# A kernel in a written order: a new order table in which the query-weight products stand behind their landing

## The chip, the cores and the metric

The kernel runs on one core of a Trainium2 chip. The metric is the device time of one execution in microseconds; the time before is the median of seven runs. Times inside an execution are counted from the start of its profiled span.

## What is computed

There are 2048 tokens of 640 numbers. Two branches read the same `x`, and a gate per token mixes them:

```python
g = sigmoid((x * gate_w).sum(-1))            # one number per token
a = linear_attention(x, wqkv, w_phi) @ wo    # 32 heads of 20
b = (silu(x @ w_gate) * (x @ w_up)) @ w_down # 1728 hidden columns
out = g * a + (1 - g) * b
```

In the attention branch q and k of each head go through a 20x20 matrix `w_phi`; the features are the softmax of the result beside the softmax of its negative (40 per head). `kv` sums feature times v over all tokens, `z` sums the features, and the result is `(phi_q kv) / (phi_q z)`. Because the sum over tokens must be complete before the first query can be finished, all key work comes ahead of the query work.

## The kernel before, in words

Everything stays in SBUF. The work is cut into items of a few microseconds. `LOADS` (line 31) and `ORDER` (line 36) are two lists of such items, and the loop at line 735 runs through them and calls the function of each; this one list fixes the order of instructions on every engine at once. Each engine then works through its own instructions strictly in that order, and `_Tracker.run` (line 143) puts a semaphore wait ahead of an instruction where it needs a result of another engine or a buffer that another engine still uses. So moving an item in the table moves its part on PE, ACT, DVE, POOL and, where it issues a transfer, on SP.

The items, with what each does on each engine:

- `H`, `G`, `X`, `U`, `V`: warm-up, gate column, transposed tokens of tiles 0 to 3, and values of a token tile. `V` (line 479) is ten matmuls on PE and two copies on ACT.
- `k0..k4` and `q0..q4` in `LOADS`: transposing DMAs on SP of the key and query columns of `wqkv` into `wT` and `wTq` (line 385), one per block of 128 rows. `t4..t15` are transposing DMAs of `x` (line 371).
- `M m`: block m of the key weights times the block-diagonal `w_phi` (`premult`, line 552), six matmuls, then a copy on DVE (m even) or ACT (m odd). `R m`: the same for the query weights from `wTq`, its copy always on ACT.
- `K t`: key features of tile t: ten matmuls, two exponentials on ACT into one of four `ekr` buffers. `S t`: sums and reciprocals on DVE. `P t`: the multiplication on POOL. `E t`: eleven matmuls that add to `kv` in PSUM.
- `I` and `N`: between them `kv` holds one PSUM pair, so only three of the four pairs are in the ring. `N` evicts `kv` on DVE. `Z` spreads `z` over partitions, `J` makes the gates, `T` copies the last 64 gate and up columns on POOL, `L` issues the loads of `wd` and `wog` on SP. `i3` and `i4` are memsets on POOL (line 405).
- `Q t`: query features, ten matmuls and two exponentials into one of three `eq` buffers. `A`, `B`, `C`: sums and denominators on DVE. `c t` (line 630): the multiplication on POOL into `ph`, and a transposing DMA on SP into `phiT`.
- `F b.k`: gate and up products of a block of four tiles, for 128 hidden columns: ten matmuls of 512 columns (five for k = 13), tanh and a copy on ACT, one operation on DVE, one on POOL.
- `O b.p`: features times `kv`, copies on ACT. `D b.u`: the down product and the output product of one token tile, 38 matmuls, the scaled copy on ACT, the output transfer on SP.

PSUM results go through a ring of pairs of banks, the pair used longest ago first:

```python
def next_pair():
    return used([r for r in ring["lru"] if r < ring["n"] and r not in held][0])
```

An item on PE thus waits until the pair that it is given has been read by ACT and DVE. And a query weight product reads what its transposing DMA wrote:

```python
pairs.append((o, (wT if which else wTq)[:, m, c, :], wbd[:, c, off:off + c1 - c0], i in (0, 3), i in (2, 5), True))
```

so PE waits there for the landing of `q m`.

Of the kernel before, what the change touches and what calls it, by code (L numbers as in the profile page):

```python
# [34 lines left out]

ORDER = """
H0 H1 H2 H3 H4 H5 H6 H7 H8 G X0 H9 H10 H11 U0.0 X1 U0.1 U1.0 U1.1 X2 U0.2 U1.2 U2.0 U2.1 X3 U2.2
U0.3 U1.3 U2.3 U0.4 U1.4 U2.4 V3 Y i3 i4 F0.0 M0 M1 F0.1 V4 M2 M3 M4 K0 K3 K1 S0 K2 S1 V7 V9 S2 P0
I V5 E0 K4 V8 P1 E1 S3 S4 P2 K5 P3 E2 P4 S5 K6 P5 R2 E3 V6 S6 K7 E4 K8 S7 E5 V14 P6 K9 E6 S8 V10
S9 P7 K10 E7 R0 K11 R4 S10 P8 E8 P9 T S11 P10 F0.5 K12 V11 P11 S12 E9 R1 F1.12 E10 K14 K13 P12 S14  # L40
P14 S13 P13 E11 R3 K15 S15 V13 F1.8 P15 F0.8 V12 V15 E12 E13 E14 E15 Q1 Q0 Q2 N A0 F1.13 F0.4 Z A1
B0 J F0.3 B1 F0.13 F1.0 C0 F1.6 F1.2 L c0 F0.6 F1.10 C1 c1 B2 F0.12 F0.10 F0.2 F1.1 A2 F0.9 C2 c2
Q3 B3 F1.5 Q4 A3 C3 c3 Q5 F1.9 F0.7 Q6 A5 A4 F1.3 B5 F1.4 F1.11 B4 O0.2 F0.11 C4 O0.0 A6 O0.1 c4
C5 Q7 B6 c5 C6 B7 c6 A7 C7 Q8 c7 F1.7 D0.2 D0.1 D0.3 Q9 Q10 D0.0 B9 O1.0 O1.1 O1.2 B8 A10 A8 A9 C8
c8 F2.5 F2.13 C9 Q11 F2.11 B10 c9 F2.12 C10 F2.0 D1.3 F2.6 A11 F2.1 F2.7 B11 F2.9 c10 Q12 Q13 A12
C11 c11 A13 F2.4 D1.2 F2.10 D1.0 Q14 B12 D1.1 O2.0 B13 C13 C12 O2.1 O2.2 c12 F3.12 A14 F3.0 F3.7
F3.4 F3.9 F3.13 F3.10 c13 Q15 F2.3 B14 A15 F2.2 F2.8 C14 F3.6 B15 C15 F3.8 F3.1 D2.2 F3.11 F3.5
c15 c14 F3.2 D2.0 D2.1 O3.0 O3.2 O3.1 F3.3 D2.3 D3.0 D3.2 D3.1 D3.3
"""


# [731 lines left out]
```

## Time and profile before

| | before |
|---|---|
| median of 7 runs | 292.06 us (291.61 to 294.35) |
| the profiled execution, its own time | 292.7 us |
| its span | 291.5 us |
| granted TensorE clock | 1.000 |
| PE matmul, busy | 286.5 us, 98% |
| DVE, ACT, POOL, busy | 159.3, 147.9, 161.3 us |
| SP's transposing loads of wTq, issued | 31.2 to 37.8 us |

PEld in the profile is the loading of matmul weights, which overlaps the matmuls. SPq is the queue of transfers that SP issues. "Idle before" is the time that an engine stood still ahead of an instruction, with the releaser behind an arrow. Since matmul records overlap, the time from the start of one item to the start of the next is the better measure of what an item costs PE.

### The profile page before, as it was taken

How to read it: one execution, taken by the hardware profiler on the slowest of the kernel's cores; microseconds unless marked ns; L12 is line 12 of the kernel's file. 1: busy time of each engine (PE TensorE's matmuls, PEld its weight loads, DVE VectorE, ACT ScalarE, POOL GpSimd, SP SyncE). 2: the span in 40 equal slices, each digit the busy share in tenths (PEclk: the TensorE clock that was granted, in tenths of full speed). 3: DMA queues.
4: the chain of work that ended last, by engine and by line, in shares of the span. 5: the costliest groups of instructions: out<-in, count | busy, mean ns of one | idle time of the engine just before them, and what ended most of it. 6: DMA issues, size and time to landing. Idle time of an engine off the chain costs nothing.

```text
span 291.5 us, 4872 instructions
## 1 busy us (share of the span) xinstructions
PE 286.5 (98%) x1975; PEld 174.8 (60%) x1975; DVE 159.3 (55%) x242; ACT 147.9 (51%) x252; POOL 161.3 (55%) x124
## 2 busy tenths in 40 slices
PE   8999989999999999999999999999999999999997
PEld 5667767675744455546775464567545455656776
DVE  1257667756677769859919793659243691100000
ACT  1358667875675557572534824543456543234112
POOL 7684977969137896765540674742345834811000
DMA  7996798000562221302360220051210200340101
GB/s 222 191 107 120 110 246 316 7 1 2 189 177 52 49 52 27 72 2 49 59 158 25 52 47 26 2 97 47 49 26 0 52 0 22 21 126 0 47 22 48
DMA packets 48777, 21.28 MB, mean 73 GB/s; under 512 B 39346, under 2 KB 48754, under 8 KB 48754
## 3 DMA queue, kind: packets, MB, share of 16 engines
q1 hardware_dynamic: 47368, 20.25, 30.9%
q10 hardware_dynamic: 1386, 0.71, 0.9%
q8 instruction: 16, 0.26, 0.4%
q14 instruction: 7, 0.06, 0.1%
HBM read 8.96 MB, written 2.62 MB: 40 GB/s over the span
## 4 chain that ended last, share of the span: by engine, by line
PE 86%; SPq 11%; DMA 1%; issue 0%; DVE 0%
PE ps L294 86%; SPq L347 10%; DMA wTq<-in_A_wqkv_dram 1%; SPq L348 1%; DVE osb L712 0%
## 5 line engine op out<-in xcount | busy, mean ns | idle before, releaser
L322 POOL TENSOR_TENSOR hT<-hT,us 128x512 bf16<-128x512 bf16 (+1 forms) x56 | 68.2, 1226 | 60.3 <-DVE hT L326 58.4
L326 DVE SCALAR_TENSOR_TENSOR hT<-hT,ps 128x512 bf16<-128x512 bf16 (+1 forms) x56 | 38.2, 684 | 69.8 <-ACT hT L312 66.3
L294 PE MATMUL ps<-xT,wg 128*128 128x512 bf16 x260 | 64.6, 379 | 0.0
L294 PE MATMUL ps<-xT,wu 128*128 128x512 bf16 x260 | 64.6, 379 | 0.0
L294 PE MATMUL ps<-wd,hT 128*128 128x320 bf16 (+2 forms) x462 | 63.9, 295 | 0.0
L312 ACT ACTIVATE hT<-ps 128x512 bf16<-128x512 f32 (+2 forms) x60 | 35.7, 595 | 45.9 <-PE ps L294 45.7
L322 POOL TENSOR_TENSOR ph<-eq,qc 128x1320 bf16<-128x1320 bf16 x16 | 40.8, 2552 | 32.0 <-DVE qc L625 29.9
L294 PEld LDWEIGHTS ps<-wd,hT 128*128 128x128 bf16 x462 | 44.5, 98 | 17.7
L294 PE MATMUL ps<-wqk,xT 128*128 128x320 bf16 x320 | 47.1, 299 | 0.0
L294 PEld LDWEIGHTS ps<-xT,wu 128*128 128x128 bf16 x260 | 25.5, 98 | 30.7
L322 POOL TENSOR_TENSOR ekr<-ekr,krec 128x1280 bf16<-128x1280 bf16 x16 | 37.5, 2357 | 8.5 <-DVE krec L336 8.1
L294 PEld LDWEIGHTS ps<-xT,wg 128*128 128x128 bf16 x260 | 25.0, 98 | 28.7 <-issue 1.7
L312 ACT ACTIVATE osb<-ps,omg 128x640 bf16<-128x640 f32 (+2 forms) x17 | 12.9, 758 | 57.0 <-PE ps L294 57.0
L294 PEld LDWEIGHTS ps<-wqk,xT 128*128 128x128 bf16 x320 | 30.6, 98 | 13.1 <-ACT hT L312 0.4
L312 ACT ACTIVATE us<-ps 128x512 bf16<-128x512 f32 (+1 forms) x56 | 33.2, 593 | 0.1
L333 DVE TENSOR_REDUCE ksum<-ekr 128x64 f32<-128x1280 bf16 x16 | 23.4, 1464 | 12.8 <-ACT ekr L312 12.8
L312 ACT ACTIVATE eq<-ps 128x640 bf16<-128x640 f32 x32 | 22.3, 703 | 16.0 <-POOL ph L322 11.1
L294 PE MATMUL ps<-wvg,xT 128*128 128x320 bf16 (+1 forms) x160 | 25.3, 306 | 0.4 <-DMA wvg<-in_A_wqkv_dram 0.3
L312 ACT ACTIVATE ekr<-ps 128x640 bf16<-128x640 f32 x32 | 22.2, 703 | 6.6 <-PE ps L294 6.1
L333 DVE TENSOR_REDUCE qz<-eq 128x64 f32<-128x1280 bf16 x16 | 23.4, 1478 | 2.6 <-ACT eq L312 2.6
L294 PE MATMUL ps<-wog,oT 128*128 128x320 bf16 (+2 forms) x165 | 24.7, 295 | 0.0
L333 DVE TENSOR_REDUCE qw<-ez 128x64 f32<-128x1280 bf16 x16 | 23.6, 1478 | 0.1
(73 smaller groups left out, 184.4 us busy)
## 6 DMA issues: line engine op xcount, KB each, us to landing
out_dram<-osb SPq DMA_DIRECT2D x15, 160.0 KB, 1.8
wd<-in_B_w_down_dram SPq DMA_DIRECT2D x1, 2080.0 KB, 9.3
wg<-in_B_w_gate_dram SPq DMA_DIRECT2D x1, 1040.0 KB, 10.6
wu<-in_B_w_up_dram SPq DMA_DIRECT2D x1, 1040.0 KB, 12.7
wg<-in_B_w_gate_dram SPq DMA_DIRECT2D x1, 800.0 KB, 6.3
wu<-in_B_w_up_dram SPq DMA_DIRECT2D x1, 800.0 KB, 8.3
wog<-in_A_wo_dram SPq DMA_DIRECT2D x2, 375.0 KB, 7.0
wvg<-in_A_wqkv_dram SPq DMA_DIRECT2D x4, 160.0 KB, 3.7
```

The lines of the kernel that those rows point to most:

```text
L294: last = pe.matmul(o, lhsT=l, rhs=r, start=st, stop=sp_, skip_group_check=sk)
L312: return run("act", lambda: act.activation(o, i, func, scale=scale), rd, [o])
L322: return run(e, lambda: eo.tensor_tensor(o, a, b, op), [a, b], [o])
L326: return run("dve", lambda: dve.scalar_tensor_tensor(out=o, in0=a, scalar=s, in1=b, op0=op0, op1=op1), rd, [o])
L333: return run("dve", lambda: dve.tensor_reduce(o, i, AX.X, ALU.add), [i], [o])
L347: return eo.dma_start_transpose(dst, src)
L348: return eo.dma_start(dst, src)
```

## The change

Only the table `ORDER` is another one. It came out of a search over such orders with a model of the engines in which the transposing DMAs take a longer pace. The items are the same, and so is everything up to `V3`, except that `i3` now stands behind `M3`. The items `R`, which read `wTq`, stood as R2, R0, R4, R1, R3 and now stand as R1, R2, R3, R0, R4, the first of them behind `E4` where it stood behind `K6`. As the whole table was searched again, nearly every other item has moved by some places too.

```
-U0.3 U1.3 U2.3 U0.4 U1.4 U2.4 V3 Y i3 i4 F0.0 M0 M1 F0.1 V4 M2 M3 M4 K0 K3 K1 S0 K2 S1 V7 V9 S2 P0
-I V5 E0 K4 V8 P1 E1 S3 S4 P2 K5 P3 E2 P4 S5 K6 P5 R2 E3 V6 S6 K7 E4 K8 S7 E5 V14 P6 K9 E6 S8 V10
-S9 P7 K10 E7 R0 K11 R4 S10 P8 E8 P9 T S11 P10 F0.5 K12 V11 P11 S12 E9 R1 F1.12 E10 K14 K13 P12 S14
-P14 S13 P13 E11 R3 K15 S15 V13 F1.8 P15 F0.8 V12 V15 E12 E13 E14 E15 Q1 Q0 Q2 N A0 F1.13 F0.4 Z A1
-B0 J F0.3 B1 F0.13 F1.0 C0 F1.6 F1.2 L c0 F0.6 F1.10 C1 c1 B2 F0.12 F0.10 F0.2 F1.1 A2 F0.9 C2 c2
-Q3 B3 F1.5 Q4 A3 C3 c3 Q5 F1.9 F0.7 Q6 A5 A4 F1.3 B5 F1.4 F1.11 B4 O0.2 F0.11 C4 O0.0 A6 O0.1 c4
-C5 Q7 B6 c5 C6 B7 c6 A7 C7 Q8 c7 F1.7 D0.2 D0.1 D0.3 Q9 Q10 D0.0 B9 O1.0 O1.1 O1.2 B8 A10 A8 A9 C8
-c8 F2.5 F2.13 C9 Q11 F2.11 B10 c9 F2.12 C10 F2.0 D1.3 F2.6 A11 F2.1 F2.7 B11 F2.9 c10 Q12 Q13 A12
-C11 c11 A13 F2.4 D1.2 F2.10 D1.0 Q14 B12 D1.1 O2.0 B13 C13 C12 O2.1 O2.2 c12 F3.12 A14 F3.0 F3.7
-F3.4 F3.9 F3.13 F3.10 c13 Q15 F2.3 B14 A15 F2.2 F2.8 C14 F3.6 B15 C15 F3.8 F3.1 D2.2 F3.11 F3.5
-c15 c14 F3.2 D2.0 D2.1 O3.0 O3.2 O3.1 F3.3 D2.3 D3.0 D3.2 D3.1 D3.3
+U0.3 U1.3 U2.3 U0.4 U1.4 U2.4 V3 Y i4 F0.0 F0.1 M0 V4 M2 M1 M3 i3 M4 K0 K1 S0 I P0 K3 S1 K2 V6 V8
+E0 K4 S3 S2 V5 P1 P3 P2 E1 V11 S4 P4 K5 V7 E2 K6 E3 K7 S5 S6 S7 E4 R1 P5 K8 R2 P6 E5 S8 V9 K9 P7
+E6 V10 P8 K10 S9 R3 E7 K11 E8 S10 R0 K12 P9 R4 P10 S11 E9 V14 K13 P11 S12 E10 K14 P12 E11 S13 P13
+K15 S14 V12 V13 P14 S15 P15 F0.6 F0.2 V15 E12 E13 E14 E15 Q2 Q0 Q1 N J T F0.13 F1.8 A0 F1.7 Z B1
+B0 F1.12 C0 c0 B2 F1.5 F1.2 F0.8 A2 C2 L Q3 F0.4 c2 A1 F1.13 F0.5 F1.6 C1 F1.1 Q5 F1.0 A3 F1.10 B3
+c1 Q4 C3 F1.9 c3 F0.7 F0.10 Q6 F0.11 F1.3 A4 F0.9 F0.12 B4 O0.1 F0.3 O0.0 C4 O0.2 B6 F1.4 c4 B5 Q7
+A6 A5 C5 c5 C6 D0.1 A7 c6 B7 C7 Q8 D0.2 D0.0 c7 A8 Q9 A9 B9 C9 Q10 F1.11 B8 c9 D0.3 C8 O1.1 B10
+A10 O1.0 O1.2 F2.6 c8 Q12 F2.3 Q11 F2.7 F2.1 B11 D1.0 C10 c10 F2.2 D1.1 A11 F2.4 Q13 C11 c11 F2.5
+A12 B13 D1.3 F2.13 F2.0 B12 C12 D1.2 A13 O2.0 O2.1 O2.2 C13 Q14 A14 c12 F2.10 F3.11 F2.12 F3.9
+F3.6 F2.9 B14 c13 Q15 F2.11 F2.8 F3.7 C14 F3.10 F3.0 B15 F3.13 A15 F3.3 F3.4 c14 C15 c15 F3.12
+F3.8 D2.2 D2.3 F3.1 F3.2 D2.0 O3.0 O3.1 O3.2 F3.5 D2.1 D3.1 D3.0 D3.2 D3.3
```

## The prediction, made before the result

> **What bounds the kernel now.** I read the page's busy shares first, then its chain, then the chain in order of time, then PE's own waits, then PE's timeline around the one wait.
>
> ```profile
> PE 286.5 (98%) x1975; PEld 174.8 (60%) x1975; DVE 159.3 (55%) x242; ACT 147.9 (51%) x252; POOL 161.3 (55%) x124
> PE 86%; SPq 11%; DMA 1%; issue 0%; DVE 0%
> ```
>
> PE is busy nearly all the time and carries 86% of the chain. The rest is the transfer queue of SP. Where the one hands over to the other, the chain in order of time shows:
>
> ```profile
> 32.52 1.28 SPq L347
> 33.79 0.04 issue
> 33.84 3.90 DMA wTq<-in_A_wqkv_dram
> 37.73 0.05 issue
> 37.78 251.66 PE ps L294 x1687
> ```
>
> The transposing load of row block 2 of the query weights, issued at 33.84, lands at 37.73. From 37.78 on PE never waits for another engine until the last matmul at 289.44. PE's own waits say the same:
>
> ```profile
> PE ps L294 <- DMA wTq<-in_A_wqkv_dram: 1.5, 1, 1.5
> PE ps L294 <- DVE ones L340: 1.1, 1, 1.1
> PE ps L294 <- DMA wvg<-in_A_wqkv_dram: 0.3, 1, 0.3
> ```
>
> The last two lie before 5 us, in a part of the order that is the same in both tables. The timeline of PE shows the first:
>
> ```profile
> 34.77 1.52 PE L294 MATMUL ps<-wqk,xT 128*128 128x320 bf16 x10
> 37.78 0.49 PE L294 MATMUL ps<-wbd,wTq 128*128 128x140 bf16 x6 [1.49 <-DMA wTq<-in_A_wqkv_dram]
> 38.10 0.51 PE L294 MATMUL ps<-v1r,ekr 128*128 128x63 bf16 x11
> ```
>
> The first row is K6, the second R2. From the start of a K tile to the start of the next item is 1.36 us everywhere else; here it is 3.01. So the wait costs 3.01 - 1.36 = **1.66 us** in start-to-start time. I laid the whole table over the start times of PE: nothing else behind K0 is over 0.1 us late (every block of O items costs 0.1 to 0.2, in both tables alike). Ahead of K0, M4 and the hand-over to K0 lose 0.10 us. The most that any order can win here is therefore about 1.66 + 0.10 = 1.76 us.
>
> One rule speaks against calling PE the bound. The page's 98% is matmul busy time, and the Trainium skill (Trainium Kernel Development and Optimization, Performance Expectations) says that this row is a bad measure because matmuls are pipelined, and that utilisation and the busy share of weight loads are the good ones. Weight loads are at 60% here; by that row up to 40% of 291.5 us, 117 us, would still be open. By start-to-start times it isn't: a gate and up pair is ten matmuls of 512 columns in 2.16 us, 216 ns each, the same 52 times over, while no start waits. The starts decide: 1.76 us, not 117.
>
> **The change, part by part.** Only the order table changes, so instructions, tiles and loads are the same, and so is the list of loads on SP. Summed with the start-to-start rows of before (F 2.16, F*.13 1.08, V 1.38, K and Q 1.36, E 0.345, M and R 0.315, D 5.17), PE's work is the same. What can differ is who waits. Times below are places on PE in the new order, summed from 12.70 (start of F0.0, everything ahead of it unchanged) plus 0.2 for the head.
>
> *R moves behind the landings.* wTq blocks 0 to 4 land at 35.1, 36.3, 37.7, 39.2 and 39.9 (the trace's landings). R1 now stands at 39.6, R2 at 41.3, R3 at 47.8, R0 at 50.1 and R4 at 51.8. The nearest is R1, 3.3 us behind its landing, so the 1.66 goes: **-1.66**. The same clock of landings covers the other loads: V6 at 25.6 needs xT of tile 6 (21.3), V8 at 27.0 needs tile 8 (23.3), M4 at 19.7 needs 18.1.
>
> *The head, F0.0 to K0.* Before: F0.0 M0 M1 F0.1 V4 M2 M3 M4 K0. After: F0.0 F0.1 M0 V4 M2 M1 M3 M4 K0. Now DVE has the casts of M0 and M2, and ACT the copies of M1 and M3, in a row just before K0 reads them. DVE: F0.1's operation of 0.69 us runs from 17.86, 0.6 later M0's cast starts, at 18.46, then come steps of 0.74: M2's cast starts at 19.22 and ends at 20.04. K0 takes M2's PSUM pair, so it starts at 20.10 and not at 19.97. ACT: V4's eviction takes 0.77 us from 18.91, M1's copy runs 19.57 to 20.28, M3's 20.2 to 20.9; K0's second chunk wants M1 at 20.37 (met), its fourth wants M3 at 20.91 (0.05 late). Sum 0.18 late, against 0.10 in the trace: **+0.08**. The bounds are 0 and 0.4, if the copies' semaphores come a tenth later each.
>
> *i3 moves from ahead of F0.0 to behind M3.* These are 4.1 us of POOL memsets and selects (2.76 for wog). They now run at about 19.9 to 24.0. POOL's next piece of work is P0, which waits for DVE's reciprocal until 25.3, so they are hidden by 1.3 us. Their neighbours on DVE are casts out of PSUM: the trace has a cast of 0.82 us inside the 3.62 us memset of ph, and 0.81 beside none, so I take 0.
>
> *The K stage.* Two F items leave it (F0.6 and F0.2 stay, four were there), E1 to E15 come closer together, and POOL's 16 multiplications at 2.36 us set its floor. From P0 at 25.4 they run without a gap to P4 at 37.3; then each waits for its reciprocal or for the one before. P_n ends and E_n starts: P0 27.8, E0 28.3; P1 30.1, E1 31.4; P2 34.9, E2 35.9; P5 40.7, E5 41.6; P6 43.7, E6 44.7; P11 56.3, E11 56.9; P15 66.1, E15 68.1. Always ahead, least by 0.5. With three PSUM pairs, ACT must clear each pair two items later: V9 at 42.0 wants R1's copy (41.6), K12 at 50.5 wants R3's (50.1), V14 at 52.5 wants R0's (52.1), K13 at 53.9 wants K12's exponentials (53.5). These R copies are 0.68 us each on ACT. Slack 0.3 to 0.4 each: **0**, at worst +0.3 each on four of them, but one late start gives the next more room, so +0.6 in all.
>
> *N, J, T and Z.* N's ten DVE operations took 74.54 to 77.66, 3.1 us behind E15. From 68.5 they end at 71.6; F0.13 needs that pair at 72.5. T's two copies end by 69.4. J now makes DVE wait for ACT from 71.8 to 74.2, with nothing due. Z at 77.9 stands 9.4 us behind E15, where it stood 7.3. **0.**
>
> *The query stage.* The tightest place that I found is Q4. C1 (2.96 us on DVE) has moved behind F1.6 and ends at 100.5, and c1 on POOL stands behind F1.10's multiplication, so it starts at 106.6. Q4's exponentials write the buffer that c1 reads; ACT stands still for them from 105.2, with F1.9, F0.7 and F0.10 queued behind. c1's row is 2.43 us, or 2.94 beside DVE work, so they start at 109.0 to 109.5 and end at 110.4 to 111.0; Q6 takes Q4's pair at 111.7. Slack 0.7 to 1.3. A rule bears on the 0.51 between the two rows: the Trainium skill (SBUF — State Buffer, Who interferes with whom) says that a DVE instruction with two SBUF inputs and a GpSimd instruction that reads SBUF exclude each other for a whole instruction. By it a 0.82 us product on DVE in the way would make c1 3.25 us, and Q6 0.4 us from late; by the rows 0.7. **0** by either.
>
> *Block ends.* D0.1 at 128.9 is now only 4.4 us behind the end of F0.3 (5.9 between F0.11 and D0.2 before). F0.3's POOL product ends at 127.2, the O0 copies on ACT at 127.9. The O items want c3's transposed tile at 120 and stand at 121.7. At the end F3.5, D2.1, D3.1 follow as F3.3, D2.3, D3.0 did; F3.5's product ends at 264.2 and is read at 267.4. **0.**
>
> *The sum.* -1.66 + 0.08 = -1.58. The profiled execution, 292.7 us with a span of 291.5, becomes 291.1 with a span of 289.9. It lies 0.6 above the median of the seven runs, 292.06; the same -1.58 on the median gives 290.5.
>
> **Rivals.** (a) *Part of it comes back.* The runs differ from the profile by 0.6, and the wait on a landing may be smaller in the median run; a late start of PE ahead of 37 us was hidden by it before and is not now; and the 0.3 us slacks of the K stage can fail. For it speaks that 0.3 us is three semaphore steps; against it that the same kind of slack held everywhere in the trace. Taking +0.6 and +0.3: 291.4. (b) *The wait only moves.* If the landings slipped with the work, R1 would wait as R2 did: 292.06. Against it: SP's queue up to there waits for nothing, and R1 has 3.3 us. (c) *A buffer becomes the bound: slower.* ACT's wait for POOL in front of the query exponentials. Before, it occurs five times, 11.1 us in all, 3.9 at the longest, and always behind enough work of PE. At Q4 only 0.7 us of cover is left in the worst reading. If c1 came 3.9 us later than I sum, PE would wait 3.9 - 0.7 = 3.2 at Q6: 290.5 + 3.2 = 293.7. It decides from the point where c1 ends behind 110.3. For it speaks that three in-order queues meet there; against it that DVE hands over C1 six microseconds before c1 starts.
>
> **How the numbers follow.** A difference under 0.5%, 1.46 us, is about what a measurement of this kernel cannot tell from none; the bounds are 290.6 and 293.5. Forecast 0.62: 290.5, from 290.0 to 291.1, so 0.45 faster and 0.17 same. Rival (a) 0.22: 0.03 faster, 0.19 same. (b) 0.05: same. (c) 0.11: 0.10 slower, 0.01 same. Together 0.48, 0.42, 0.10. The range reaches from 289.9, the bound of 1.76 with the spread of the runs, to 292.3, which takes in (a) and (b).
>
> **What would show it.** Right: no PE wait on wTq, the chain one PE piece from near the head on, R1 near 39.6, K1 near 21.5, Q6 near 111.7, a span near 289.9. Wrong: a PE gap at K0 over 0.4 (the head), at K12, V14 or K13 (ACT's copies), at Q6 (c1), or at D0.1 (F0.3).

## The result and the profile after

| | before | changed |
|---|---|---|
| median | 292.16 us (60 runs, 290.97 to 294.9) | 290.47 us (25 runs, 289.94 to 292.82) |
| changed / before | | 0.9938, 95% interval 0.9922 to 0.9954 |
| the profiled execution, its own time | 292.7 us | 290.81 us |
| its span | 291.5 us | 289.6 us |
| start of F0.0, of K0, of R2 on PE | 12.70, 20.05, 37.78 us | 12.13, 19.56, 40.72 us |

The forecast was 290.5. The page of the changed kernel, busy shares and chain:

```profile
PE 285.9 (99%) x1975; PEld 174.6 (60%) x1975; DVE 165.3 (57%) x242; ACT 147.7 (51%) x252; POOL 160.6 (55%) x124
PE 97%; DMA 1%; SPq 0%; DVE 0%; issue 0%
```

PE had 86% of the chain and SP's queue 11%; now SP's queue has less than half a percent. Where the hand-over lies is in the chain in order of time (start, length, what):

```profile
1.74 4.23 DMA wvg<-in_A_wqkv_dram
6.01 1.12 PE ps L294 x6
7.41 0.55 PE ps L294 x4
7.99 0.72 PE ps L294 x4
8.99 278.27 PE ps L294 x1914
```

PE's last wait on a transfer is now that for the second block of the value weights, at 6.0 us, and its unbroken piece begins at 8.99 instead of 37.78. PE's own waits in the changed kernel, whole:

```profile
PE ps L294 <- DVE ones L340: 1.1, 1, 1.1
PE ps L294 <- DMA wvg<-in_A_wqkv_dram: 0.2, 1, 0.2
```

The row with wTq is gone. The timeline of PE around K6, which took 3.01 us to the next start, and around R1 and R2:

```profile
35.64 1.52 PE L294 MATMUL ps<-wqk,xT 128*128 128x320 bf16 x10
36.99 0.51 PE L294 MATMUL ps<-v1r,ekr 128*128 128x63 bf16 x11
...
39.04 0.48 PE L294 MATMUL ps<-wbd,wTq 128*128 128x140 bf16 x6
39.36 1.52 PE L294 MATMUL ps<-wqk,xT 128*128 128x320 bf16 x10
40.72 0.48 PE L294 MATMUL ps<-wbd,wTq 128*128 128x140 bf16 x6
```

K6 takes 1.35 to the next start, and R1 and R2 stand 4.9 and 4.2 us behind their landings, which in this execution were 34.1 and 36.5.

Laid over each other item by item, the two profiles differ on PE by -1.65 at K6, by -0.57 ahead of F0.0, where the order is the same, and by +0.06 from F0.0 through K0; every other kind of item sums to within 0.01. From the last matmul to the end of the span it is 2.30 us where it was 2.03. Together -1.65 - 0.57 + 0.06 + 0.28 = -1.9, the whole difference of the spans. Of this the change has made 1.59. The 0.57 lies where the two orders are the same, so it is a difference between two executions; that the 0.28 is one too is taken, not shown.

### The profile page after: what moved, and what is told of

Its sections match the earlier page's. It is cut to its first block, busy times and chain, and to the rows that moved or that the text cites. A ratio compares the mean times of both kernels' runs of the same rounds, so it can differ in the third digit from the quotient of the medians.

```text
span 289.6 us, 4875 instructions
## 1 busy us (share of the span) xinstructions
PE 285.9 (99%) x1975; PEld 174.6 (60%) x1975; DVE 165.3 (57%) x242; ACT 147.7 (51%) x252; POOL 160.6 (55%) x124
## 4 chain that ended last, share of the span: by engine, by line
PE 97%; DMA 1%; SPq 0%; DVE 0%; issue 0%
PE ps L294 97%; DMA wvg<-in_A_wqkv_dram 1%; SPq L348 0%; PE ps L306 0%; DVE osb L712 0%
## 5 line engine op out<-in xcount | busy, mean ns | idle before, releaser
L322 POOL TENSOR_TENSOR hT<-hT,us 128x512 bf16<-128x512 bf16 (+1 forms) x56 | 69.0, 1239 | 77.7 <-DVE hT L326 77.5
L312 ACT ACTIVATE hT<-ps 128x512 bf16<-128x512 f32 (+2 forms) x60 | 35.8, 597 | 41.1 <-PE ps L294 40.8
L322 POOL TENSOR_TENSOR ph<-eq,qc 128x1320 bf16<-128x1320 bf16 x16 | 39.3, 2456 | 16.2 <-DVE qc L625 12.4
L294 PE MATMUL ps<-wqk,xT 128*128 128x320 bf16 x320 | 47.7, 299 | 0.0
L333 DVE TENSOR_REDUCE ksum<-ekr 128x64 f32<-128x1280 bf16 x16 | 23.4, 1461 | 9.6 <-ACT ekr L312 9.6
```

Of the source, the lines that this page charges most:

```text
L294: last = pe.matmul(o, lhsT=l, rhs=r, start=st, stop=sp_, skip_group_check=sk)
L312: return run("act", lambda: act.activation(o, i, func, scale=scale), rd, [o])
L322: return run(e, lambda: eo.tensor_tensor(o, a, b, op), [a, b], [o])
L333: return run("dve", lambda: dve.tensor_reduce(o, i, AX.X, ALU.add), [i], [o])
```

## The experiments

The theory (A): the wait of R2 for its landing was the whole gain; before, PE's time ahead of that landing was hidden, and now it isn't. The rivals: the rest of the new table is what helps (B), the wait only moves (C), or a buffer is now so near to binding that it gives part back.

**One item moved.** In the order of before, R2 alone goes behind E4.

```
-... K6 P5 R2 E3 V6 S6 K7 E4 K8 ...
+... K6 P5 E3 V6 S6 K7 E4 R2 K8 ...
```

> The order of before, with one item moved: R2 stands behind E4 instead of behind K6. Theory A (the wait of R2 for the landing of its block of wTq is the whole gain): PE reaches R2 near 39.5 us, behind the landing near 37.7, no wait is left and the time is that of the change, 290.5 us (1.6 below before). Rival B (the gain comes from the rest of the newly searched table, in the head and the stages): most of it is missing, 291.5 to 292.1 us. Rival C (the wait only moves to R0 or another load): a wait of PE on wTq stays in the trace, 292.1 us.

Measured 290.68 us against 291.72 for before on the same chip, ratio 0.9966 (0.9945 to 0.9986). PE's timeline in it, from K6 to R2:

```profile
34.63 1.52 PE L294 MATMUL ps<-wqk,xT 128*128 128x320 bf16 x10
35.99 0.51 PE L294 MATMUL ps<-v1r,ekr 128*128 128x63 bf16 x11
...
39.41 0.48 PE L294 MATMUL ps<-wbd,wTq 128*128 128x140 bf16 x6
```

No wait on wTq is left, and the time is near that of the whole new table, 290.47. The gain is 1.0 us (the interval is 0.4 to 1.6) and not 1.6, mostly since before itself took 0.4 less on this chip than in the result; the changed kernel was run again beside before on one chip, further down.

**The load moved instead of the work.** The order of before, with another list of loads:

```
-... t15 q0 q1 q2 q3 q4 f1 f2
+... t15 q2 q0 q1 q3 q4 f1 f2
```

> The order of before, unchanged; only the list of loads is another one: the transposing load of block 2 of wTq is issued ahead of those of blocks 0 and 1, which moves its issue from about 33.8 to 31.2 us and its landing from about 37.7 to 35.1 us, while R2 stands at 36.1. Theory A: the wait is gone without any moved work, 290.5 us. Rival B (only a later place of the work helps, or the queue hands the first block over late anyhow): 292.1 us.

Measured 290.52 us, ratio 0.9968 (0.9941 to 0.9996), a gain of 1.2 (0.1 to 1.7 by the interval). Block 2 now lands at 34.1, and R2 runs in its old place straight behind K6:

```profile
34.95 1.52 PE L294 MATMUL ps<-wqk,xT 128*128 128x320 bf16 x10
36.30 0.48 PE L294 MATMUL ps<-wbd,wTq 128*128 128x140 bf16 x6
```

One load moved two places ahead does, as far as these runs can tell, as much as a new table. Together with the run before it, and with the item-by-item comparison above, where no other kind of item behind F0.0 than K6 and those of the head sums to more than about 0.01, this speaks against B: no other part of the new table is needed for a gain of this size.

**More work in the head, before and after.** Twenty more matmuls of 128 columns ahead of F0.0, in both kernels; their result is overwritten by F0.0, so nothing of the output changes.

```
+    def pad():
+        b = 2 * [r for r in ring["lru"] if r < ring["n"] and r not in held][0]
+        mm([(bank(b, 0, P), ones[:, :], ones[:, :], True, True, False)] * 20)
-... U2.4 V3 Y ...
+... U2.4 V3 W Y ...
```

> The order of before with 20 more matmuls of 128 columns on PE ahead of F0.0, about 1.1 us of work whose result is overwritten. Theory A (before, PE is early for the landing by 1.66 us and whatever it loses ahead of it is hidden): no difference, 292.1 us, and the wait of R2 shrinks from 1.66 to about 0.55. Rival (PE's own work bounds the kernel from the start in both): 1.1 more, 293.3 us.

> The changed kernel with the same 20 matmuls ahead of F0.0. Theory A (in the changed kernel nothing hides the head of PE any more): the whole 1.1 us shows, 291.6 us. Rival (a landing or a buffer still bounds the changed kernel): less than half of it, below 291.0 us.

Before with them: 291.90 us, ratio 1.0014 (0.9992 to 1.0036, which is -0.2 to +1.0 us): 1.1 us of PE's work cost nothing that can be measured. In the profile the wait on wTq hasn't shrunk to 0.55, it is gone: block 2 landed at 36.2 in this execution, and PE came at 36.5. Changed with them: 291.72 us, ratio to before 1.0000 (0.9980 to 1.0019), so about 1.0 to 1.25 above the changed kernel on other chips (290.71 and 290.47), and 1.0 to 1.2 above the two kernels without the wait on this chip (290.68 and 290.52). Nearly all of it shows. The two kernels with the added work, neither of which waits on wTq in its profile, take the same time. So before was bound by the landing, which hid work ahead of it up to the length of the wait, and in the changed kernel nothing hides it.

**R2 put back too early.** The changed kernel with R2 behind K5:

```
-... P4 K5 V7 E2 K6 E3 ... K8 R2 P6 E5 ...
+... P4 K5 R2 V7 E2 K6 E3 ... K8 P6 E5 ...
```

> The changed kernel with one item moved back: R2 stands behind K5, where PE comes to it near 34.3 us (33.9 in the profile of the changed kernel), ahead of its landing between 36.5 and 37.7. Theory A (the place of R2 against its landing alone sets the loss): PE waits 2.5 to 3.4 us and the time is 293.0 to 293.9 us. Rival B (the new table is faster for other reasons): 290.5 us.

Measured 294.47 us, ratio 1.0092 (1.0058 to 1.0125). PE's timeline in the profile, an execution of 292.65 us, with K5 and R2:

```profile
32.20 1.52 PE L294 MATMUL ps<-wqk,xT 128*128 128x320 bf16 x10
36.14 0.49 PE L294 MATMUL ps<-wbd,wTq 128*128 128x140 bf16 x6 [2.42 <-DMA wTq<-in_A_wqkv_dram]
```

K5 takes 3.94 instead of 1.36, a loss of 2.6, and the landing at 36.1 sets the start of R2. That is the theory's size. The median is over the top of what was expected, and the granted clock goes with it: three runs at 1.000 took 292.65 to 293.41 us, four at 0.994 took 294.47 to 296.35.

**The old head.** The changed kernel with the head of before.

```
-V3 Y i4 F0.0 F0.1 M0 V4 M2 M1 M3 i3 M4 K0 ...
+V3 Y i3 i4 F0.0 M0 M1 F0.1 V4 M2 M3 M4 K0 ...
```

> The changed kernel with the head of before: i3 i4 F0.0 M0 M1 F0.1 V4 M2 M3 M4, the memsets of i3 ahead of F0.0 again. The sum of the prediction: 0.08 us less, too little to be measured, so 290.5 us; in the profile the stalls from F0.0 to K0 are 0.10 us instead of 0.17. Rival (the memsets on POOL beside the casts on DVE cost something): 0.3 us less or more.

Measured 290.57 us, ratio to before 0.9962 (0.9950 to 0.9974), against 290.47 and 290.71 for the changed kernel: no difference. From the start of F0.0 to that of K1 it is 8.73 us here and 8.79 in the changed kernel. Neither the new head nor the memsets of i3 beside the casts cost anything to speak of.

**The tight buffer.** The changed kernel with a memset of a dead buffer on POOL ahead of c1.

```
-... A3 F1.10 B3 c1 Q4 ...
+... A3 F1.10 B3 i5 c1 Q4 ...
+            memset("pool", v1r[:, 0:5, :], 0.0)    # i5
```

> The changed kernel with a memset of 3465 columns of a dead buffer on POOL just ahead of c1, about 2.97 us by the rows of the other memsets (0.86 ns a column). In the profile of the changed kernel Q4's exponentials end 0.65 us ahead of Q6, which takes their pair of banks. Theory (c1 on POOL holds Q4's exponentials on ACT, and these hold Q6 on PE, with 0.65 us of cover): PE waits 2.97 - 0.65 = 2.3 us at Q6 and the time is 292.8 us. Rival (there is more cover than that row shows): 290.5 to 291.0 us.

Measured 294.19 us, ratio 1.0073 (1.0043 to 1.0102). ACT's timeline shows Q4's exponentials waiting behind c1, then PE's shows Q6, the two halves of F0.11 behind it, and the start of the next item:

```profile
111.93 1.44 ACT L312 ACTIVATE eq<-ps 128x640 bf16<-128x640 f32 x2 [7.38 <-POOL ph L322]
```

```profile
113.43 1.72 PE L294 MATMUL ps<-wqk,xT 128*128 128x320 bf16 x10 [2.16 <-ACT eq L312]
114.94 2.34 PE L294 MATMUL ps<-xT,wg 128*128 128x512 bf16 x5
117.07 1.73 PE L294 MATMUL ps<-xT,wu 128*128 128x512 bf16 x5
118.64 1.24 PE L294 MATMUL ps<-xT,wg 128*128 128x512 bf16 x5
```

The memset took 2.98 us and Q6 came 2.32 late, so the cover was 0.66, the 0.65 of the row. But the five matmuls of 512 columns in the second row took 2.13 us to the next start instead of 1.08. The table by stretches says why (from:to, length, busy time of each engine, clock, DMA):

```profile
111.00:114.00 3.00, 0.84 (x7) 0.43 (x6) 0.39 (x2) 2.04 (x4) 0.84 (x1) 1.00 0.33 65
114.00:118.00 4.00, 4.00 (x16) 1.75 (x14) 1.95 (x3) 2.31 (x5) 3.34 (x2) 0.58 0.22 42
118.00:124.00 6.00, 6.00 (x29) 2.72 (x28) 2.98 (x4) 4.32 (x8) 4.72 (x5) 1.00 0.31 60
```

After the wait the granted clock fell to half for 3.4 us (0.58 over four microseconds is 1.68 lost), and from the start of Q6 to that of the item behind F0.11 it was 5.21 us (113.43 to 118.64) instead of 3.52, so the clock cost 1.7 more. The runs split by it: three at a clock of 1.000 took 292.72 to 292.89 us, which is the 2.3 that was expected, and four at 0.994 took 294.19 to 294.99.

**The changed kernel again, and a shorter head.** The last two ran on one chip, beside before. In the second, the transposes of the head come earlier:

```
-... H11 U0.0 X1 U0.1 U1.0 U1.1 X2 U0.2 U1.2 U2.0 U2.1 X3 U2.2
+... H11 X1 U0.0 U1.0 U0.1 U1.1 X2 U0.2 U1.2 X3 U2.0 U2.1 U2.2
```

> The changed kernel itself, on one chip beside the kernel of before and the next variant, since the gains of single items moved (1.0 to 1.2 us) were measured against a kernel of before that was faster on those chips. Theory (the gain is the landing minus the place of R2, which differs from chip to chip, while the changed kernel does not depend on it): about 290.5 us, 1.0 to 1.3 below before. Rival (the whole table is worth more than the one item moved): 1.6 to 1.7 below before.

> The changed kernel with the first row of its table changed: X1 ahead of U0.0, U1.0 ahead of U0.1, and X3 ahead of U2.0, so that PE has the next token tile transposed when a block of the value weights lands. Theory (nothing hides the head of PE any more, so idle time between 4.5 and 8.5 us that can be filled is won whole): 0.3 to 0.5 us less than the changed kernel, about 290.0 us. Rival (the first loads bound the head, and the transposes only wait for them earlier): no difference, 290.5 us, or worse by the wait for a late token tile.

The changed kernel: 290.71 us against 291.85, ratio 0.9952 (0.9932 to 0.9972), a gain of 1.1 by the medians, 0.8 to 2.0 by the interval. One item and one load moved gained 1.0 and 1.2 against before on their chip, so by the medians the whole table is not worth more than R2's move; the intervals would leave room for some tenths. The shorter head: 290.36 us, ratio 0.9939 (0.9914 to 0.9963). It is 0.35 below its neighbour, in the expected direction, but the two intervals overlap by most of their width: not settled. In its profile F0.0 starts 3.5 us behind the last landing of a value block (8.8), in the changed kernel's first profile 4.1 (8.0).

The profile of this second execution of the changed kernel also shows how open its head now is. F0.0 starts at 13.74 instead of 12.13, 1.61 later; the last matmul ends at 288.86 instead of 287.25, 1.61 later. The first row is PE's timeline of that run, the second the same six matmuls in the first profile:

```profile
6.21 1.78 PE L294 MATMUL ps<-wvg,xT 128*128 128x320 bf16 x6 [0.39 <-DMA wvg<-in_A_wqkv_dram]
```

```profile
6.01 1.12 PE L294 MATMUL ps<-wvg,xT 128*128 128x320 bf16 x6 [0.19 <-DMA wvg<-in_A_wqkv_dram]
```

Its head matmuls came 0.27 us apart until about 9.9 us, those of the first profile 0.14 apart from 6.4 on. This execution left no record of the clock, so that its clock was still at half is an inference from the factor of two. It is backed by the five profiles that have a record (the changed kernel's first one, and those of the one item moved, the old head, the tight buffer and the shorter head): there the record of full rate begins at 5.4 to 7.3 us, at 6.27 in the first of these, and the spacing of matmuls of one width falls by half at that very place.

## Why the prediction was right

*R behind the landings, -1.66.* Right: K6 gave back 1.65, no R waits, and moving R2 alone or its load alone gives the same time. Its size is not a constant, though. It is the landing of block 2 minus PE's place, and the landing ranged from 35.8 to 37.7 us over the profiles with the loads in their old order. The profile that I read had the latest landing of them, so its 1.66 is at the upper end. Pooled over all runs the gain is 1.69; beside the same chip's runs of before it was 1.1. So the mechanism was right, but that the median came within 0.03 of 290.5 is in part luck: one execution's wait was put on a median of seven runs, and against before on one chip the gain was a third smaller. Why the pooled runs show more is open. Ten of the 60 runs of before took 293.9 to 294.9 us, with none between 292.89 and 293.9 and none of the changed kernel's 25 above 292.82; without these ten the median of before is 292.04 and the gain 1.6, so they don't explain it, and their clocks aren't on record.

*The head, +0.08.* Measured +0.06 against the trace. The parts weren't all where I put them: M3 starts 0.08 late, M4 0.09, and K0 adds nothing for M2's cast or M3's copy. Sum 0.17, where 0.18 was worked out.

*i3 hidden.* Right: i3 ended at 23.4, P0 started at 24.8, and the old head gives the same time.

*The K stage, 0.* Right, with the slacks as summed: P0 ended 0.59 ahead of E0 (0.5), P5 0.86 ahead of E5 (0.9), P11 0.57 ahead of E11 (0.6); and ACT's copies of R freed the pairs of V9, K12 and V14 0.44 ahead, where 0.3 to 0.4 was the sum.

*The query stage, 0.* Right. These lines of the changed kernel's timeline are Q4's exponentials and Q6:

```profile
109.00 1.44 ACT L312 ACTIVATE eq<-ps 128x640 bf16<-128x640 f32 x2 [4.46 <-POOL ph L322]
111.09 1.11 PE L294 MATMUL ps<-wqk,xT 128*128 128x320 bf16 x7
```

The exponentials end at 110.44 and Q6 starts at 111.09: 0.65 of cover, just under the 0.7 to 1.3 that I gave. c1 took the short 2.42; what was late was F1.10's product ahead of it on POOL, 1.67 us where most of these products take 1.15. POOL's rows, and DVE's beside them, show why:

```profile
104.86 1.67 POOL L322 TENSOR_TENSOR hT<-hT,us 128x512 bf16<-128x512 bf16 x1 [0.75 <-DVE hT L326]
106.49 2.42 POOL L322 TENSOR_TENSOR ph<-eq,qc 128x1320 bf16<-128x1320 bf16 x1
```

```profile
104.70 0.82 DVE L322 TENSOR_TENSOR ez<-eq,zb 128x1280 bf16<-128x1280 bf16 x1
107.07 1.92 DVE L326 SCALAR_TENSOR_TENSOR qw<-qz,qw 128x64 f32<-128x64 f32 x1
```

F1.10's product started 0.16 us behind a DVE product of two SBUF tiles and took 0.52 longer. Then c1 held DVE: the next operation with two SBUF inputs took 1.92 and ended at 108.99, just behind c1 at 108.91. In the run with the tight buffer the same operation ran beside the memset, which reads nothing, and took 0.22. So the exclusion that the prediction weighed for c1 is real, but it struck one item earlier, and it cost 0.5 a time and not the 0.82 of the whole DVE product: in both profiles each of the 22 products of these two kinds that took 0.5 longer overlaps such a DVE product.

*Block ends, 0.* Right: no D item started late.

*The step that was loose* is in the sum's frame: "everything ahead of it unchanged", so 12.70 for F0.0. The order ahead of F0.0 is unchanged, its time isn't: 12.13 and 13.74 in two profiles of the same kernel. Before, that was hidden behind the landing, and rival (a) named it. It decides how a single execution comes out (the profile lost 1.9 us instead of 1.58); what it does to the median was not separated from the wait.

*The rivals.* (a) came half true: the smaller wait in other executions is real, and the exposed head too. (b), the wait moves, fell: R1 came 4.9 us behind its landing. (c), the buffer, had its mechanism right, and nearly its point: c1 later by more than 0.66 us stops PE. What it lacked was the clock: a wait of 2.3 us cost 1.7 us more than it lasted.

## What to carry to other kernels

When an engine is busy for 98% of the span, lay its start times against the usual spacing: the one wait that is left may be all there is to win, and moving one item, or one load, past it wins it. Take the size of a wait on a transfer from several executions, because a landing can move by more than a microsecond (35.8 to 37.7 here) and the loss is landing minus place. Once such a wait is gone, what lay hidden ahead of it counts in full, so look there next.

## What the runs showed of the hardware

A wait of PE of 2.3 us went, in four of the seven runs with the tight buffer, with a mean granted clock of 0.994; the one of them that was traced has the clock at half for 3.413 us behind the wait, and the median of the four is 1.6 us above that of the three at 1.000. So it went with the wait of 2.6 us where R2 was put back too early, four of seven too; there the traced execution kept its clock. The wait of 1.66 us left the clock at 1.000 in the profile of before, and the starts behind it keep their usual spacing; of the 72 runs of before beside my kernels, one, at 294.03 us, had 0.994. The Trainium skill (TensorE: Matmul & The Clock Gate, What's actually happening) gives a free-running window of 3413 ns, which is the very length seen, and says that the clock drops after at least one idle window. Here PE stood still for only about two thirds of that length, and the clock still dropped in most runs. The traces show the grid: with the tight buffer the full rate had lasted 109.226 us, 32 times 3.413, when it fell at 114.63, and in four other profiles it lasted 283.306 us, 83 times, and fell after the kernel's last matmul. In the one length of 3.413 ahead of the fall at 114.63, PE had worked for 1.25 us; in that ahead of the other four falls, for 0.4 to 1.1. So a window need not be idle from end to end. That it depends on how the wait lies to this grid would explain why the same kernel does both; no run here varied it alone.
